# Transposes moved from TensorE to VectorE in a chunk-attention and FFN kernel, with slots of 256 tokens and a new order of the first loads

## The chip, the cores and the metric

The kernel runs on one core of a Trainium2 chip. The metric is the device time of one execution in microseconds (us). A run counts as slow when it took over 1.5 % longer than the fastest of its kernel. Each set of runs was made beside runs of the kernel before on the same chip.

## The reference

Attention is taken within chunks of 64 tokens, for 8 batches, 8 heads, 576 tokens and a head size of 64. The result, as 4608 tokens of 512, goes through a multiplicative FFN.

```python
scores = scale * np.matmul(q_c, k_c.transpose(0, 1, 2, 4, 3))   # 64 x 64 per chunk and head
attn = softmax(scores)
x = matmul(attn, v_c)            # then 4608 x 512
a = x @ w1                       # 512 -> 1024
b = x @ w2
h = a * b @ w3                   # 1024 -> 1024
return h @ w_out                 # 1024 -> 512
```

Both kernels form `w3o = w3 · w_out` once (1024 x 512) and then `(a * b) @ w3o`. They work in bf16, with f32 sums.

## The kernel before

It works in slots of 128 tokens. TensorE turns q, k and x with transposes against an identity, in 64x64 pieces. VectorE copies the turned pieces out of the PSUM tiles that TensorE wrote (`qkT<-pa`, 691 ns each for 128x1024; `xt<-pb`, 424 ns for 128x512).

```python
def do_slot(xu=None, tu=None, su=None, pu=None):        # cut
    if xu is not None:
        ...  tr(xv[half[g], r, n, :], xn[...], ident[half[r], half[r]])   # x: 16 transposes
    if tu is not None:
        ...  tr(tv[half[g], r, s, n, :], qk[...], ident[half[r], half[r]])  # q and k
    if su is not None:
        ...  mm(sv[...], lhsT=qkT[half[r], ci, 1, ...], rhs=qkT[half[r], ci, 0, ...])  # scores
    if pu is not None:
        ...  mm(pb[...], lhsT=e[half[t], ...], rhs=vbuf[...])             # values
    ...
    nc.scalar.activation(e, pa, Exp, scale=scale)
    nc.vector.tensor_copy(qkT_t[tu], tv)
    nc.vector.tensor_copy(xt[...], xv)
    nc.vector.reciprocal(rc, pv[..., D:D + 1]); nc.vector.tensor_mul(xn, pv[..., 0:D], rc)
```

The loads and the front come in this order: w3 and w_out first, with `w3o` formed as they land, and q, k of the first slots between; then w1 and w2; then a and b.

```python
load_w3(0, 1); ...; load_w(wo, ...); load_to(1); ...; load_w3(6, 8)
for w, ap in ((w1, moe_w1), (w2, moe_w2)): ...load_w(...)
load_to(5); load_v(1); load_to(9)
do_w3T(0); do_w3T(1); do_w3o(0); do_slot(tu=0); do_w3o(1); do_slot(tu=1, su=0)   # cut
...
do_w3o(7)
... # then do_a, do_b, do_o with slots placed between
```

The softmax here doesn't subtract the row's maximum and nothing guards it: scores larger than these inputs give would overflow.

## Time and profile before

| | before |
|---|---|
| time, median of 3 (lowest to highest) | 271.62 us (270.75 to 272.07) |
| span of the profiled execution | 270.6 us |
| TensorE, VectorE, ScalarE, GpSimd busy | 90, 45, 34, 35 % |
| first `a` matmul | 43.06 us |

A busy share is an average over the whole span. The row of 40 slices is therefore the first thing to read (slices are counted from 0). The prediction below shows that row, the chain of waits for the first 66 us, and the steady stage. A piece is a start, a length and what filled it; "issue" is time in which TensorE waited for nothing that the profile shows.

```profile
76.56 1.60 issue
...
83.06 1.03 issue
```

### The profile page before, as it was taken

To read this page: it belongs to the slowest core of one execution; us is meant where nothing else is said; L and a number is where in the kernel's file an instruction comes from. 1 tells how busy PE (TensorE), PEld (TensorE's weight loads), DVE (VectorE), ACT (ScalarE), POOL (GpSimd) and SP (SyncE) were. 2 spreads that over 40 slices of the span, in tenths; PEclk is the share of its full clock that TensorE was granted. 3 is DMA by queue.
4 is the path that set the end of the run, shared out by engine and by line. 5 is a ranking of instruction groups with operands and counts; after the bars stand their busy time and mean duration, and the time that the engine had idled before them with its cause. 6 is when DMAs were issued, how large, how long until landed. Compare 5 with 4: busy or idle time off the path is not lost.

```text
span 270.6 us, 8708 instructions
## 1 busy us (share of the span) xinstructions
PE 242.6 (90%) x3896; PEld 127.0 (47%) x3936; DVE 121.4 (45%) x235; ACT 91.2 (34%) x161; POOL 93.9 (35%) x113
## 2 busy tenths in 40 slices
PE   1198599999867999999999999999999999999994
PEld 1135454445655655454444454444444544444441
DVE  1113560364556546775555445555454454332210
ACT  1003125322433343443433344433433343233331
POOL 8484327988857077555422520000000000000000
PEclk9999799999999999999999999999999999999998
DMA  5999999999999999999997991211111111111223
GB/s 87 166 175 169 210 204 158 156 156 202 200 157 142 65 124 155 172 77 151 115 95 84 102 143 45 76 43 41 41 41 41 41 41 70 47 41 39 78 78 118
DMA packets 121620, 29.39 MB, mean 109 GB/s; under 512 B 112880, under 2 KB 115952, under 8 KB 121584
## 3 DMA queue, kind: packets, MB, share of 16 engines
q0 software_dynamic: 116400, 19.41, 94.3%
q1 hardware_dynamic: 5184, 9.44, 9.4%
q8 instruction: 31, 0.51, 0.8%
q14 instruction: 5, 0.04, 0.0%
HBM read 38.80 MB, written 9.44 MB: 178 GB/s over the span
## 4 chain that ended last, share of the span: by engine, by line
PE 78%; DMA 10%; issue 3%; DVE 3%; POOL 2%; ACT 2%; ACTq 0%; POOLq 0%
PE a_ps L59 22%; PE b_ps L59 21%; PE o_ps L59 21%; DMA w_76<-in_moe_w_dram 4%; DMA wo<-in_moe_w_out_dram 4%; PE pa L62 3%; PE pb L62 3%; PE wp L59 3%; DMA out_dram<-o_sb 2%; PE pa L59 2%; PE pb L59 2%; DVE qkT L165 1%; POOL qk L65 1%; DVE xn L175 1%; PE w3tp L62 1%
## 5 line engine op out<-in xcount | busy, mean ns | idle before, releaser
L202 DVE TENSOR_TENSOR ab<-a_sb,b_ps 128x512 bf16<-128x512 f32 (+1 forms) x80 | 50.1, 630 | 57.4 <-PE b_ps L59 52.3
L59 PE MATMUL b_ps<-xt,w_75 128*128 128x512 bf16 (+1 forms) x316 | 74.1, 357 | 0.8 <-ACT o_sb L214 0.3
L59 PE MATMUL a_ps<-xt,w_74 128*128 128x512 bf16 (+1 forms) x294 | 72.3, 357 | 1.6 <-issue 0.5
L59 PE MATMUL o_ps<-w3o,ab 128*128 128x512 bf16 x283 | 66.7, 379 | 0.5 <-issue 0.3
L194 ACT COPY a_sb<-a_ps 128x512 f32<-128x512 f32 (+1 forms) x80 | 43.4, 543 | 49.8 <-PE a_ps L59 47.4
L65 POOL DMA_DIRECT2D qk<-in_q_dram x40 | 34.1, 854 | 46.7 <-PE pa L59 21.9
L59 PEld LDWEIGHTS <-w_75 128*128 128x128 bf16 x320 | 31.1, 98 | 31.4 <-issue 0.8
L214 ACT COPY o_sb<-o_ps 128x512 f32<-128x512 f32 x36 | 21.1, 586 | 66.8 <-PE o_ps L59 62.1
L59 PEld LDWEIGHTS <-ab 128*128 128x128 bf16 x288 | 27.6, 98 | 32.6
L59 PEld LDWEIGHTS <-w_74 128*128 128x128 bf16 x320 | 28.6, 98 | 26.4
L65 POOL DMA_DIRECT2D qk<-in_k_dram x40 | 34.2, 858 | 5.6 <-DMA w_76<-in_moe_w_dram 3.6
L165 DVE COPY qkT<-pa 128x1024 bf16<-128x1024 bf16 x36 | 24.9, 691 | 20.1 <-PE pa L62 13.6
L168 DVE COPY xt<-pb 128x512 bf16<-128x512 bf16 x36 | 15.3, 424 | 40.8 <-PE pb L59 38.1
L160 ACT ACTIVATE e<-pa 128x512 bf16<-128x512 f32 x36 | 21.5, 598 | 28.9 <-PE pa L59 27.1
L175 DVE TENSOR_TENSOR xn<-pb,rc 128x512 bf16<-128x512 f32 x36 | 24.8, 690 | 1.0
L59 PE MATMUL wp<-wo,w3T 128*128 128x512 bf16 x59 | 16.6, 427 | 6.4 <-DMA wo<-in_moe_w_out_dram 5.4
L62 PE MATMUL pa<-ident,qk 64*64 64x64 bf16 x1152 | 16.2, 196 | 1.5 <-issue 1.0
L62 PEld LDWEIGHTS <-qk 64*64 64x64 bf16 x1152 | 12.9, 111 | 6.0 <-issue 5.8
L62 PEld LDWEIGHTS <-xn 64*64 64x64 bf16 x576 | 7.5, 108 | 16.0 <-issue 9.9
L62 PE MATMUL w3tp<-ident,w_76 128*128 128x128 bf16 x64 | 6.4, 265 | 9.5 <-DMA w_76<-in_moe_w_dram 9.5
L233 ACT CAST w3o<-wp 128x512 bf16<-128x512 f32 x8 | 4.7, 586 | 29.9 <-PE wp L59 29.9
L62 PE MATMUL pb<-ident,xn 64*64 64x64 bf16 x576 | 11.6, 199 | 1.9 <-DVE xn L175 1.7
(27 smaller groups left out, 93.6 us busy)
## 6 DMA issues: line engine op xcount, KB each, us to landing
out_dram<-o_sb SPq DMA_DIRECT2D x36, 256.0 KB, 2.9
qk<-in_q_dram POOLq DMA_DIRECT2D x32, 128.0 KB, 6.5
qk<-in_k_dram POOLq DMA_DIRECT2D x32, 128.0 KB, 6.4
vbuf_80<-in_v_dram POOLq DMA_DIRECT2D x6, 288.0 KB, 8.5
vbuf_81<-in_v_dram POOLq DMA_DIRECT2D x6, 288.0 KB, 6.8
vbuf_82<-in_v_dram POOLq DMA_DIRECT2D x4, 288.0 KB, 7.0
w_76<-in_moe_w_dram POOLq DMA_DIRECT2D x4, 256.0 KB, 7.9
wo<-in_moe_w_out_dram POOLq DMA_DIRECT2D x1, 1024.0 KB, 10.6
```

The costliest lines, as they stand in the source:

```text
L59: return inorder(nc.tensor.matmul(*a, **kw))
L62: return inorder(nc.tensor.transpose(*a, **kw))
L65: return inorder(nc.gpsimd.dma_start(dst, src))
L160: nc.scalar.activation(e[:].rearrange("p r m c q -> p r (m c q)"), pa[:, :, 0:HW], Exp, scale=scale, bias=0.0)
L165: nc.vector.tensor_copy(qkT_t[tu][:].rearrange("p r s n t -> p r (s n t)"), tv.rearrange("p r s n t -> p r (s n t)"))
L168: nc.vector.tensor_copy(xt[:, :, xu * UT:(xu + 1) * UT].rearrange("p n (r t) -> p r n t", r=2), xv)
L175: nc.vector.tensor_mul(xn[:], pv[:, :, :, 0:D], rc.to_broadcast([P, 2, NHP, D]))
L194: nc.scalar.copy(a_t[j][:, 0:n], a_ps[:, 0:n])
L202: nc.vector.tensor_mul(ab_t[t][:, j, 0:n], a_t.pop(j)[:, 0:n], b_ps[:, 0:n])
L214: nc.scalar.copy(o_sb[:], o_ps[:])
L233: nc.scalar.copy(w3o[:, ko, :], wp[:])
```

## The change

The intent has three parts. First, TensorE's transposes go away: VectorE turns q, k, x (and w3) by 32x32 blocks in one instruction each, and the index order of the tiles is chosen so that blocks suffice. Second, slots become "pairs" of 256 tokens and every PSUM tile has two banks, in a ring of four. Third, the front is turned round: two pairs of q, k, v come first, then w1 and w2 by quarters, and a and b are formed while w_out and w3 load; later, a and b run two stages behind the values. The diff, cut to its core:

```diff
-    ident = consts.tile([P, P], bf, name="ident")
+    def psum(name):
+        return ps.tile([P, 2, 512], f32, tag="p", name=name)        # bufs=4
...
-                            tr(tv[half[g], r, s, n, :], qk[...], ident[half[r], half[r]])
-            nc.vector.tensor_copy(qkT_t[tu][:]..., tv...)
+        inorder(nc.vector.transpose(
+            qkT_t[p][:, s].rearrange("p e h (y t) -> p h t e y", t=2),
+            qk_t[p][:, s].rearrange("p h (t e y) -> p h t e y", t=2, e=2)))
...
+                for i in range(NB):                                  # scores, 32-row blocks
+                    mm(s_t[p][half[i % 2], i // 2, h * CH:(h + 1) * CH],
+                       lhsT=qkT[blk[i], 1, e, h, :],
+                       rhs=qkT[blk[i], 0, e, h, :], start=(e == 0), stop=(e == 1))
...
-    load_w3(0, 1)
-    load_w(wo, moe_w_out, 0, DM)
-    ...
+    load_to(1)
+    load_w12(0); load_w12(1); load_w12(2)
+    load_to(2)
+    load_w12(3)
+    load_to(4)
+    load_wo()
+    load_w3(0, DF // BL // 2); load_w3(DF // BL // 2, DF // BL)
+    load_to(6)
...
+    T_(0); S_(0); T_(1); P_(0); N_(0); X_(0); S_(1); P_(1); N_(1); X_(1)
+    for j in range(2):
+        do_ab(0, j)(); do_ab(1, j)()
+    do_ab(0, 2)()
+    T_(2); S_(2); do_ab(1, 2)(); P_(2); N_(2); do_ab(0, 3)(); X_(2); do_ab(1, 3)()
+    T_(3); do_ab(2, 0)(); S_(3); ...        # and so on to pair 4
+    for j in range(4):
+        do_ab(4, j)(); do_w3T(j)
+    T_(5); do_w3o(0); do_w3o(1); ...
```

T turns q and k, S is scores and exp, P values, N the division by the sum, X turns x. One `do_ab` is a quarter of a and b of a pair: 16 matmuls of 256 columns, a copy on ScalarE, and the product on VectorE, which the call `()` places.

## The prediction

> **What bounds the kernel now.** I read the page first: the busy shares and the 40 slices (6.77 us each).
>
> ```profile
> span 270.6 us, 8708 instructions
> ...
> PE 242.6 (90%) x3896; PEld 127.0 (47%) x3936; DVE 121.4 (45%) x235; ACT 91.2 (34%) x161; POOL 93.9 (35%) x113
> ...
> PE   1198599999867999999999999999999999999994
> ...
> DMA  5999999999999999999997991211111111111223
> ```
>
> TensorE is the bound from slice 12 on; VectorE and ScalarE have more than half of their time free. The loss is at the front and in slices 10 and 11, where the DMA row stands at 9. So next the chain of waits, in order of time, for the first 66 us:
>
> ```profile
> 3.04 10.65 DMA wo<-in_moe_w_out_dram
> ...
> 18.61 11.30 DMA w_76<-in_moe_w_dram
> ...
> 43.06 4.53 PE a_ps L59 x21
> ```
>
> The first `a` matmul starts at 43.06 us: the kernel first loads w3 (w_76 here) and w_out and forms w3·w_out. Then the steady part, in the timeline of TensorE (start, length, group):
>
> ```profile
> 159.65 1.89 PE L59 MATMUL o_ps<-w3o,ab 128*128 128x512 bf16 x8
> 161.47 0.32 PE L62 MATMUL pb<-ident,xn 64*64 64x64 bf16 x16
> 161.61 0.43 PE L62 MATMUL pa<-ident,qk 64*64 64x64 bf16 x32
> 161.87 0.31 PE L59 MATMUL pa<-qkT 64*64 64x64 bf16 x16
> 161.99 0.32 PE L59 MATMUL pb<-vbuf_82,e 64*64 64x65 bf16 x16
> 162.24 1.04 PE L59 MATMUL a_ps<-xt,w_74 128*128 128x512 bf16 x3
> 163.12 1.03 PE L59 MATMUL b_ps<-xt,w_75 128*128 128x512 bf16 x4
> 163.98 1.03 PE L59 MATMUL a_ps<-xt,w_74 128*128 128x512 bf16 x4
> ```
>
> No gap: from 163.12 to 163.98 four matmuls of 512 columns take 0.86 us, 215.9 ns each. The eight `o` matmuls are issued by 161.38 (159.65 + 8 x 0.2159), the next `a` starts at 162.24: an attention slot of 128 tokens costs TensorE 0.86 us for 80 small matmuls, 48 of them transposes. From start to start these take 8 to 9 ns each ((161.87 - 161.61)/32 = 8.1), in all 0.65 us; the other 0.2 us is at entry (0.09) and exit (0.12). The 256-column form, which becomes the only one for a and b, is in the same view:
>
> ```profile
> 72.14 0.60 PE L59 MATMUL b_ps<-xt,w_75 128*128 128x256 bf16 x4
> ...
> 73.01 0.60 PE L59 MATMUL b_ps<-xt,w_75 128*128 128x256 bf16 x4
> ```
>
> Eight of them in 0.87 us: 109 ns each. Last, the groups, for what VectorE and the DMA queue pay:
>
> ```profile
> L202 DVE TENSOR_TENSOR ab<-a_sb,b_ps 128x512 bf16<-128x512 f32 (+1 forms) x80 | 50.1, 630 | 57.4 <-PE b_ps L59 52.3
> ...
> L65 POOL DMA_DIRECT2D qk<-in_q_dram x40 | 34.1, 854 | 46.7 <-PE pa L59 21.9
> ...
> L165 DVE COPY qkT<-pa 128x1024 bf16<-128x1024 bf16 x36 | 24.9, 691 | 20.1 <-PE pa L62 13.6
> L168 DVE COPY xt<-pb 128x512 bf16<-128x512 bf16 x36 | 15.3, 424 | 40.8 <-PE pb L59 38.1
> ```
>
> [...]
>
> **The change, part by part.**
>
> *TensorE.* Removed: 1152 + 576 transposes of q, k and x and 64 of w3. The matmuls that remain are cut smaller: scores of 256 tokens are 64 matmuls on 32-row blocks (before 32), values 64 on 32-column blocks (before 32). At the old 8.1 ns, 128 of them are 1.04 us; there are three changes of mode (128 to 64x32, to 32x64, to 128) at about 0.1: 0.32. Estimate 1.36 us for 256 tokens, against 2 x 0.86 = 1.72. Over 18 pairs -6.5 us. The w3 transposes: 64 at some 60 ns, -3.8. a and b: before 512 at 215.9 ns and 128 at 109.2 = 124.5; after 1152 at 109.2 = 125.8, +1.3. o (288 x 215.9 = 62.2) and w3·w_out (64 x 215.9 = 13.8) stay. Sum before 124.5 + 62.2 + 13.8 + 3.8 + 36 x 0.86 = 235; after 125.8 + 62.2 + 13.8 + 18 x 1.36 = 226. So the removed transposes alone are worth 9 us.
>
> *VectorE.* Estimates [...]: a q or k transpose (1024 elements) 1.22 us, an x transpose (512) 0.69, a w3 one 1.22. A pair then costs 2 x 1.22 + 2 x (0.20 + 0.69) for reciprocal and scaling + 2 x 0.69 + 4 x 0.69 = 8.4 us; in all 18 x 8.4 + 8 x 1.22 = 161 us, from 121. In the steady stage TensorE needs 1.36 + 64 x 0.1092 + 16 x 0.2159 = 11.8 us, so VectorE at 8.4 lies beside it. I followed one stage through the built order: values and scores, normalising and turning the values, four a,b groups with the next q and k between, then o. With a and b two stages behind, x was turned a stage earlier; o's ScalarE copy (1.02 us, as 512 elements are 586 ns and 256 are 373) ends just inside the 1.36 us of small matmuls before its PSUM slot is wanted. No wait is left, or one of 0.1 us.
>
> *Loads.* A q or k issue is 131 KB and 0.86 us, and from 41 to 62 us POOL issues nearly without a pause while the stretch moves 157 GB/s; the weight stretch (34 to 41 us) moves 203. So I take the small loads to be held by issuing. After, a q or k issue copies 256 tokens in the same 1024 runs, now twice as long: four issues or 3.5 us for a pair of 786 KB, 224 GB/s. Then 203 GB/s holds, 3.9 us for a pair and 1.3 for a weight quarter of 262 KB.
>
> *The front.* The first load lands 3.6 us after its issue at 1.26 (from before). Then, estimated: q0, k0 at 5.0 and 6.3, pair 1 at 11.5, the first quarters of w1 and w2 at 14, the last at 26, pairs 2, 3, 4 at 23, 30, 33, w_out 39, w3 49. VectorE turns q0, k0 until 7.6; scores, exp, values until 10.7; it turns pair 1 until 11.5, scales pair 0 until 13.4 and turns it until 15. So a and b start at about 15 instead of 43 us, and form while w3 loads. But in this front everything alternates on two engines in program order, and TensorE waits for VectorE: for q and k of pair 2, which stand behind a product on VectorE (3.4 us), of pair 3 and for x of pair 2 (2.5), of pair 4 (2), others 0.7: 8.6 us, and the first matmuls run at 427 ns for 512 columns, as w3·w_out does in before from 13.7 to 17: 1.7 more.
>
> *Sum.* Start 15; 20 groups of a,b for pairs 0 to 4 at 1.75 = 35; three pairs' attention 4.1; waits 10.3: 64.5. w3·w_out, pair 5's attention and o(0): 18.6: 83. Stage 6 (scores, a,b, two o) 14.6, stage 7 8.3: 106. Ten stages of 11.8: 224. The last values, a,b and o: 11.2, then a,b 7.0 and two o 6.9: 249. Before, the last matmul group ends at 266.76 and the span at 270.6, a tail of 3.84 that stays: 253. The median of before is 1 us above its page: 254; I take 253, since the waits at the front are rounded up.
>
> **Rivals.** (1) The block transposes run at half the assumed rate, because their rows are strided. Then VectorE needs some 12 us in a stage of 11.8 and becomes the bound, and the front grows by about 6: 266 to 270. [...] (2) Small matmuls on 32-row or 32-column tiles don't overlap as the 64x64 ones do: at 16 ns a pair costs 1 us more, 18 in all: 270. For it: twice as many, each with its own weight load[...]. (3) Loads stay at 157 GB/s: w3 lands at 62 instead of 49 while it is wanted at 58: +4. The w3 and w_out loads go to 32 partitions each, which nothing in the trace tells of. (4) The front overlaps better than I have it and the waits behind VectorE are short: 246.
>
> **Range and chances.** Rival 4 sets the low end, rival 3 with a little of 1 or 2 the high end: 244 to 264. Faster by over 2% means below 266.2; only rival 1 or 2 in full prevents it, about one in ten together. Slower needs both.
>
> **What would show it.** The first a,b group near 15 us; transposes of 1024 elements near 1.22 us and of 512 near 0.69; VectorE busy about 161 us; a stage of 11.8 us late in the run without gaps; 1.36 us between the last o and the first a,b matmul; gaps before the scores of pairs 2, 3, 4 ended by VectorE. A transpose above 1.8 us, or more than 2 us of small matmuls in a stage, makes the prediction wrong, as would a first a,b group after 22 us.

The 1.22 us for turning 1024 elements, and with it the 8.4 us of a pair and the 161 us in all, were an estimate: the trace of before has no such instruction and does not show its rate. The nearest that was measured there is the product of L202 over 128x512, 684 ns with the forms kept apart, against the 0.69 us used for 512 elements.

## The result, and the profile after

The changed kernel took 268.58 us (median of 4 runs, 266.13 to 269.19). The kernel before took 271.41 us in the same rounds (4 runs). The ratio is 0.9867, with a 95 % interval of 0.9817 to 0.9916. Here and below a ratio is taken from the fast runs of the same rounds, so it is not quite the ratio of the medians quoted. By the 2 % bar this counts as the same time. 253 was predicted, with a range of 244 to 264: the prediction was wrong by 15.6 us.

The page of the changed kernel, in the rows that answer to those of before: the busy shares, the slices (of 6.68 us), the instruction queue, and five groups (count, then busy us and mean ns of one).

```profile
span 267.3 us, 8283 instructions
...
PE 234.8 (88%) x3791; PEld 170.2 (64%) x3808; DVE 154.6 (58%) x231; ACT 84.0 (31%) x114; POOL 84.5 (32%) x112
...
PE   0369477974899999999999999999999999999993
...
PEclk9999979997999999999999999999999999999998
DMA  8999999999999979799989791202202020210204
...
q8 instruction: 30, 0.49, 0.8%
...
L188 DVE TENSOR_TENSOR ab<-a_sb,ab_ps 128x512 bf16<-128x512 f32 x72 | 48.4, 673 | 56.4 <-ACT a_sb L187 56.3
...
L129 DVE STREAM_TRANSPOSE qkT<-qk 128x1024 bf16<-128x1024 bf16 x36 | 46.1, 1297 | 3.2 <-DMA qk<-in_q_dram 3.0
...
L170 DVE STREAM_TRANSPOSE xt<-xn 128x512 bf16<-128x512 bf16 x36 | 23.3, 686 | 0.0
...
L58 PE MATMUL pv<-vbuf,e 64*32 64x96 bf16 x1152 | 14.0, 215 | 8.4 <-issue 6.1
```

From slice 11 on TensorE is full, and its busy time fell by 7.8 us. Slices 0 to 10 are mostly thin: TensorE works early now, but with holes. The clock row has two dips, in slices 5 and 9. The last line says that the values waited 6.1 us for "issue", which means for nothing that the profile shows.

The timeline of TensorE shows the front, and a steady stage below it. Columns: start, length, group, and in brackets the idle time before it and what ended that.

```profile
17.12 0.65 PE L58 MATMUL pv<-vbuf,e 64*32 64x96 bf16 x33 [1.27 <-issue]
17.70 11.53 PE L58 MATMUL ab_ps<-xt,w 128*128 128x256 bf16 x80
33.00 0.86 PE L58 MATMUL s_ps<-qkT 32*64 32x64 bf16 x64 [3.77 <-DVE qkT L129]
33.79 3.35 PE L58 MATMUL ab_ps<-xt,w 128*128 128x256 bf16 x16
37.07 0.69 PE L58 MATMUL pv<-vbuf,e 64*32 64x96 bf16 x61
39.27 0.22 PE L58 MATMUL pv<-vbuf,e 64*32 64x96 bf16 x3 [1.51 <-issue]
39.42 3.67 PE L58 MATMUL ab_ps<-xt,w 128*128 128x256 bf16 x32
...
60.04 0.68 PE L58 MATMUL pv<-vbuf,e 64*32 64x96 bf16 x60
64.07 0.27 PE L58 MATMUL pv<-vbuf,e 64*32 64x96 bf16 x4 [3.35 <-issue]
64.27 5.22 PE L58 MATMUL ab_ps<-xt,w 128*128 128x256 bf16 x32
70.35 7.16 PE L58 MATMUL ab_ps<-xt,w 128*128 128x256 bf16 x64 [0.87 <-DVE xt L170]
77.35 2.97 PE L58 MATMUL w_ps<-wo,w3T 128*128 128x512 bf16 x12
...
154.66 0.72 PE L58 MATMUL pv<-vbuf,e 64*32 64x96 bf16 x64
155.32 0.71 PE L58 MATMUL s_ps<-qkT 32*64 32x64 bf16 x64
155.96 7.16 PE L58 MATMUL ab_ps<-xt,w 128*128 128x256 bf16 x64
162.95 3.62 PE L58 MATMUL o_ps<-w3o,ab 128*128 128x512 bf16 x15
166.50 0.72 PE L58 MATMUL pv<-vbuf,e 64*32 64x96 bf16 x64
```

The steady stage is as predicted: 166.50 - 154.66 = 11.84 us (predicted 11.8), 155.96 - 154.66 = 1.30 us for values and scores (predicted 1.36), no gap. The front is not: w3·w_out starts at 77.35 us where 64.5 was worked out, 12.9 us late, and from there to the end nothing is lost. Values stop three times in mid-burst on "issue" (1.27, 1.51 and 3.35 us), behind 31 of 64 matmuls of pair 1, at 61 of 64 of pair 2, at 60 of 64 of pair 4. And 16 a,b matmuls take 3.35 us at 33.79, where 16 take 1.92 in full clock (at 32.43 in the run "warm" below).

What these stops are, the records of the DMA packets tell. The queue q8 that the page calls "instruction" moved 30 packets of 16384 bytes (0.49 MB). The page counts 7599 instructions of TensorE (3791 matmuls and 3808 weight loads), 253 for each packet; 30 times 256 would be 7680. So I took each packet for a block of some 256 of TensorE's instructions. I set the start of each packet against TensorE's records, both from the trace, and counted TensorE's own instructions (a weight load and a matmul are two) up to each stop:

```
kernel   instructions   packet of   TensorE    from packet to
         before stop    16 KB at    goes on    going on
after        446          14.79       17.12       2.33
after        956          36.86       39.27       2.41
after       1722          61.58       64.07       2.49
before      1982          75.71       78.17       2.46
before      2238          81.68       84.09       2.41
```

Each stop ends 2.3 to 2.5 us after such a packet starts. With 66 added (one constant, chosen to fit), the counts are 512, 1022, 1788, 2048 and 2304, within 4 of multiples of 256. Counted by TensorE's records in the trace, semaphore records among them, no constant is needed: the three stops of the changed kernel come behind record 449, 961 and 1729, which are 2 x 256 and 3 x 256 apart. The three stops last 6.1 us together, and 21, 32 and 35 packets of the loads were in flight at the start of the three instruction packets. So theory A was: **TensorE runs out of its instruction block**, because 256 instructions are used up in a burst of attention (128 for the scores, 128 for the values of a pair in 0.65 us each) sooner than the next block comes through the loads. How long a block takes can be read off too. From the moment at which the records pass such a boundary to the start of the next packet it is 2.2 to 4.0 us at the seven boundaries of the first 65 us, with 21 to 36 load packets in flight; some 2.4 us later TensorE could go on.

The half speed is in the granted clock: two stretches of 3.41 us at 0.5, at 33.35 and 64.07, after the idle times of 3.77 and 3.35 us. The idle time in front of a stretch was not always that long: it was 2.77 us in pad128 (stretch at 50.98) and 1.97 in gate5 (at 38.74), two of the runs below.

Rival theories were: **B**, the stops come from something in the values themselves or their buffers, not from where the block ends; **C**, the loss is VectorE's order alone (the wait of 3.77 us at 33.00) and the clock that falls behind it; **D**, the early a and b are not worth anything, and the front loses what it gains however it is fed. The first two were settled; D was not.

### The profile page after: what moved, and what is told of

Read it like the earlier page. It is cut to its first block, busy times and chain, and to the rows that moved or that the text cites. A ratio compares the mean times of both kernels' runs of the same rounds, so it can differ in the third digit from the quotient of the medians.

```text
span 267.3 us, 8283 instructions
## 1 busy us (share of the span) xinstructions
PE 234.8 (88%) x3791; PEld 170.2 (64%) x3808; DVE 154.6 (58%) x231; ACT 84.0 (31%) x114; POOL 84.5 (32%) x112
## 4 chain that ended last, share of the span: by engine, by line
PE 79%; DMA 6%; DVE 5%; POOL 5%; issue 3%; ACT 1%; ACTq 0%; POOLq 0%
PE ab_ps L58 42%; PE o_ps L58 23%; PE w_ps L58 5%; DMA w<-in_moe_w_dram 4%; PE pv L58 4%; PE s_ps L58 4%; DVE qkT L129 3%; DMA qk<-in_q_dram 2%; POOL w L61 2%; POOL qk L61 1%; DVE xt L170 1%; POOL vbuf L61 1%; DVE ab L188 1%; ACT a_sb L187 1%; ACT o_sb L200 0%
## 5 line engine op out<-in xcount | busy, mean ns | idle before, releaser
L58 PE MATMUL ab_ps<-xt,w 128*128 128x256 bf16 x1152 | 135.3, 280 | 2.6 <-DVE xt L170 2.6
L58 PEld LDWEIGHTS <-w 128*128 128x128 bf16 x1152 | 113.8, 100 | 19.9 <-DVE xt L170 3.4
L188 DVE TENSOR_TENSOR ab<-a_sb,ab_ps 128x512 bf16<-128x512 f32 x72 | 48.4, 673 | 56.4 <-ACT a_sb L187 56.3
L187 ACT COPY a_sb<-ab_ps 128x512 f32<-128x512 f32 x72 | 42.1, 585 | 97.7 <-PE ab_ps L58 97.7
L129 DVE STREAM_TRANSPOSE qkT<-qk 128x1024 bf16<-128x1024 bf16 x36 | 46.1, 1297 | 3.2 <-DMA qk<-in_q_dram 3.0
L61 POOL DMA_DIRECT2D vbuf<-in_v_dram x40 | 33.8, 857 | 19.6 <-PE pv L58 14.3
L200 ACT COPY o_sb<-o_ps 128x1024 f32<-128x1024 f32 (+1 forms) x19 | 18.3, 968 | 49.6 <-PE o_ps L58 49.6
L58 PE MATMUL s_ps<-qkT 32*64 32x64 bf16 x1152 | 13.6, 199 | 15.9 <-DVE qkT L129 15.9
L166 DVE TENSOR_TENSOR xn<-pv,rc 128x512 bf16<-128x512 f32 x36 | 24.9, 692 | 1.2
L145 ACT ACTIVATE e<-s_ps 128x1024 bf16<-128x1024 f32 x18 | 18.4, 1024 | 21.0 <-PE s_ps L58 21.0
L58 PEld LDWEIGHTS <-qkT 32*64 32x64 bf16 x1152 | 11.5, 111 | 18.6 <-DVE qkT L129 17.0
L170 DVE STREAM_TRANSPOSE xt<-xn 128x512 bf16<-128x512 bf16 x36 | 23.3, 686 | 0.0
```

The lines of the kernel that those rows point to most:

```text
L58: return inorder(nc.tensor.matmul(*a, **kw))
L61: return inorder(nc.gpsimd.dma_start(dst, src))
L129: inorder(nc.vector.transpose(qkT_t[p][:, s].rearrange("p e h (y t) -> p h t e y", t=2), qk_t[p][:, s].rearrange("p h (t e y) -> p h t e y ...
L145: inorder(nc.scalar.activation(e_t[p][:].rearrange("p u h q -> p u (h q)"), s_t.pop(p)[:], Exp, scale=scale, bias=0.0))
L166: inorder(nc.vector.tensor_mul(xn_t[p, u][:], pv[:, :, :, 0:D], rc.to_broadcast([P, 2, 4, D])))
L170: inorder(nc.vector.transpose(xt[:, :, t0:t0 + UT].rearrange("p o (m y) -> p m o y", y=BL), xn_t.pop((p, u))[:].rearrange("p r (c n) (z o) ...
```

## The experiments

Twelve sets of runs were made, two of them repeats. All gave correct results. w3·w_out start is the first `w_ps` matmul in the profiled run; half-clock stretches are counted in pieces of 3.41 us between 25 and 95 us, behind the cold start (in the changed kernel the first 25 a,b matmuls, from 17.70 to 23.0 us, start 213 ns apart; from 23.2 us on they start 109 apart).

| run | us, median (lowest to highest) | ratio to before [95 %] | w3·w_out at | "issue" in front of s_ps, pv, ab_ps | half-clock stretches |
|---|---|---|---|---|---|
| changed kernel | 268.58 (266.13 to 269.19) | 0.9867 [0.9817, 0.9916] | 77.4 | 6.1 | 2 |
| pad64 | 261.75 (261.24 to 262.02) | 0.9624 [0.9594, 0.9655] | 69.2 | 1.4 | 1 |
| pad128 | 265.05 (263.81 to 266.20) | 0.9733 [0.9682, 0.9783] | 74.5 | 4.2 | 3 |
| pad30 | 262.14 (261.95 to 262.38) | 0.9639 [0.9623, 0.9655] | 70.5 | 1.7 | 1 |
| warm | 260.00 (259.78 to 260.81) | 0.9567 [0.9535, 0.9600] | 68.1 | 1.5 | 0 |
| gate5 | 264.33 (263.17 to 265.69) | 0.9723 [0.9678, 0.9769] | 73.9 | 3.6 | 2 |
| order_a | 264.08 (260.22 to 264.70) | 0.9602 [0.9522, 0.9682] | 72.7 | 8.1 | 3 |
| order_a_pad64 | 255.78 (254.50 to 256.18) | 0.9372 [0.9334, 0.9409] | 63.8 | 1.2 | 1 |
| order_b | 254.98 (254.10 to 256.52) | 0.9353 [0.9300, 0.9405] | 63.8 | 1.8 | 0 |
| order_b again | 254.44 (254.32 to 254.76) | 0.9358 [0.9344, 0.9372] | 62.6 | 1.7 | 0 |
| w3_first | 271.42 (270.56 to 273.04) | 0.9960 [0.9916, 1.0005] | 16.3 | 1.6 | 4 |
| w3_first_b | 260.66 (260.24 to 260.89) | 0.9574 [0.9544, 0.9604] | 16.4 | 0 | 1 |
| w3_first_b again | 262.89 (one run, state unknown) | none | 16.3 | 0.2 | 2 |

(The kernel before took 271.41 us beside the changed kernel, 271.8 beside pad64, pad128, warm and gate5, 271.91 beside pad30 and the repeat of order_b, 272.8 beside the orders and w3_first, 271.87 beside w3_first_b. Two of order_a's four runs were slow, and its last three columns are from a slow one.)

### pad64: every block boundary moved by 64 instructions

Thirty-two tiny matmuls on constants (64 TensorE instructions) stand before everything else, while TensorE would wait for the first q and k anyway. Nothing reads their result.

```diff
+    def pad(n):
+        t = psum("pad")
+        for _ in range(n):
+            mm(t[0:BL, 0, 0:BL], lhsT=vbuf[0][0:BL, 0, 0, D:VW],
+               rhs=vbuf[0][0:BL, 0, 0, D:VW], start=True, stop=True)
+    pad(32)
     load_to(1)
```

> 32 dummy 32x32 matmuls at the very start, before anything is loaded: 64 more TensorE instructions, which shift every later block of 256 instructions by 64. Theory A (the three stops of 1.3, 1.5 and 3.35 us inside the values of pairs 1, 2 and 4 are waits for the next block of 256 TensorE instructions, which comes about 6.3 us after the last block was begun while the loads keep the queues full): the stops leave these three places; with the new phase at most one of about 0.3 us is left at pair 1, so w3*w_out begins near 70 instead of 77.4 us and the time falls by 5 to 8 us, to about 262. Theory B (the stops belong to these instructions: a v load, a PSUM slot or small matmuls as such): the three stops stay where they are and the time stays within 1.5 us of 268.

The time fell to 261.75 us, and w3·w_out starts at 69.2. The waits of TensorE (engine, line and what it waited for; us in total, times, longest) have no values on "issue" any more; what is left stands in front of the last of pair 1's 64 scores. It is 1.2 us, where about 0.3 was expected at pair 1:

```profile
PE s_ps L58 <- DVE qkT L129: 13.5, 5, 6.1
...
PE s_ps L58 <- issue: 1.2, 1, 1.2
```

The kernel does more work and is 7 us faster. The values did not change. Their buffers did, by one place: the dummies take one tile of the ring in PSUM, so every later tile moves on by one. But pad30, pad64 and pad128 all move the ring by this one tile and stop in different places, so with the two runs below B falls. One of the two half-clock stretches went with the long stop at pair 4.

### pad128: the same, twice as far

```diff
+    pad(64)
```

> The same with 64 dummy matmuls, a shift of 128 instructions. Theory A: the stops in the values of pairs 1, 2 and 4 are gone, but new ones stand inside the scores of pair 1 (about 1.6 us) and at the end of the values of pair 3 (about 3 us), where none was; time about 264 to 267. Theory B: stops at pairs 1, 2 and 4 as before, none at the other two places, 268.

It took 265.05 us. The stops came where the boundaries now are:

```profile
PE pv L58 <- issue: 2.8, 1, 2.8
...
PE s_ps L58 <- issue: 1.4, 1, 1.4
```

The stop in the values is now pair 3's, a gap of 2.98 us between weight loads after instruction 1466 (1466 + 66 = 1532), and the other is in the scores of pair 1. The same dummies twice over cost 3.3 us against pad64, and only the place of the boundary differs. Three stretches of half clock (30.50 to 37.33 and 50.98 to 54.40) are part of that.

### gate5: fewer loads in flight when pair 4's block is asked for

The loads of pair 5 and later are held back until pair 4's values are scaled, by one column that VectorE writes into pair 5's tile.

```diff
     load_w3(DF // BL // 2, DF // BL)
-    load_to(6)
 ...
     N_(4)
+    qk_t[5] = io.tile([P, 2, H, 2 * D], bf, tag="qk", bufs=6, name="qk")
+    inorder(nc.vector.memset(qk_t[5][:, :, 0, 0:1], 0.0))
+    load_to(6)
```

> The loads of pair 5 and later are held back until pair 4's values have been scaled, by a VectorE write of one column into pair 5's buffer, so that no load is in flight around 57 to 61 us. Theory A with its second half (the block comes late because the loads fill the same queues): the block wanted in pair 4's values is fetched about 1.5 us after the last one was begun instead of 3.9, as late in the run, where no load is in flight; the stop of 3.35 us shrinks below 1.5 us or goes, with it the half-clock window after it; w3*w_out begins 3 to 5 us earlier; the time is about 264, unless pair 5's loads then come late for the w3*w_out stage (they need 4 us and are wanted 15 us later). If blocks always come that slowly after a burst: the stop stays at 3.3 us and the time at 268.

264.33 us. The blocks in question started at 59.68 and 63.20 with no load packet in flight, and pair 4's stop shrank from 3.35 to 0.36 us, with the same instructions at the same boundaries:

```profile
62.17 0.22 PE L58 MATMUL pv<-vbuf,e 64*32 64x96 bf16 x4 [0.36 <-issue]
```

The sum over the whole run, as us in total, times and longest:

```profile
PE pv L58 <- issue: 3.6, 3, 2.0
```

What is left beside it is pair 1's (1.3) and pair 2's (2.0, before 1.5). From passing the boundary to the packet's start it was 0.94 and 1.03 us at these two blocks, and 2.5 to 4.0 at the five before them in the same run, with 18 to 38 load packets in flight. So both halves of theory A hold in the one case tried: TensorE stopped where the boundary was, and the block's packet started later, by 1.5 to 3 us, when loads were in flight.

### warm: TensorE kept busy while it waits for VectorE

Fifteen 512-column matmuls on data that are there fill the 3.77 us wait in front of pair 2's scores.

```diff
     do_ab(0, 2)()
+    warm(15)        # 15 x mm(t[:, 0, :], lhsT=w1[:, 0, 0:P], rhs=xt[:, 0:2, 0:PT])
     T_(2)
```

> 15 dummy matmuls of 512 columns in the gap of 3.8 us before the scores of pair 2, nothing waits for them. If the slow a,b group after the gap (3.29 us instead of 1.77) is the granted clock falling to half after TensorE stood idle, that group takes 1.8 us, the half-clock window at 33.35 us is gone from the trace, and w3*w_out begins 1.5 us earlier; the time falls by about 1.5 us to 267 (the shift of 30 instructions may move a stop of theory A by some tenths). If the group is slow for its operands (xt just turned, weights just landed), it stays at 3.3 us and the time stays.

It took 260.00 us, a gain of over 8 us where 1.5 was expected. The half-clock stretch is gone: the first a,b group behind pair 2's scores takes 1.92 us instead of 3.35.

```profile
27.84 3.40 PE L58 MATMUL warm<-xt,w 128*128 128x512 bf16 x15
31.80 0.71 PE L58 MATMUL s_ps<-qkT 32*64 32x64 bf16 x64 [0.55 <-DVE qkT L129]
32.43 1.92 PE L58 MATMUL ab_ps<-xt,w 128*128 128x256 bf16 x16
34.28 0.72 PE L58 MATMUL pv<-vbuf,e 64*32 64x96 bf16 x64
```

But the stop in pair 2's values is gone as well, and pair 4's is 0.23. The fifteen dummies are 30 instructions: they moved the boundaries, and the block's packet started at 30.47 instead of 36.86. The experiment mixed two causes; alone it tells nothing about the clock's worth.

### pad30: the same 30 instructions, without the warm-up

```diff
+    pad(15)
     load_to(1)
```

> 15 dummy 32x32 matmuls (30 TensorE instructions) before everything else, so that every later block boundary comes 30 instructions earlier, as behind the warm-up of the run before, but with no long matmuls in the gap before the scores of pair 2. It tells the two effects of the warm-up run apart. Theory A (instruction blocks): the block that ran out in the values of pair 2 is now asked for before the wait for VectorE at about 30.5 us, so that stop (1.5 us) and the one of pair 4 (3.35 us, and the half-clock stretch after it, 1.65 us) go or shrink below 0.5, while the half-clock stretch at 33 to 37 us stays: about 261.5 us, w3 times w_out at 70 to 71. Then the clock was worth about 1.5 us in the warm-up run (260.0). Rival (the clock was the cause of the whole gain there): this run stays at 267 to 269 us.

262.14 us, with w3·w_out at 70.5 and a half-clock stretch at 32.50, as expected under A. The waits keep pair 1's stop and 0.3 of pair 4's:

```profile
PE pv L58 <- issue: 1.7, 2, 1.4
```

So 30 instructions' shift gives some 6.4 us of the warm run's gain (268.58 - 262.14), and the clock about 2.1 (262.14 - 260.00; on two chips, where the runs of the kernel before differ by 0.1). In the profiled runs 0.8 us of this is the cold start (the first five a,b groups take 11.09 us in pad30, 10.30 in warm), which the warm-up cannot have changed. C as the whole cause falls; the clock is a part of it.

### order_a and order_a_pad64: VectorE's order, and the boundary again

The calls of the front are put in another order, found with a small model of the queues that knew nothing of instruction blocks: q and k of pairs 2, 3 and 4 are turned before the products that kept them waiting. The same instructions, no dummies; order_a_pad64 adds `pad(32)`.

```diff
-    do_ab(0, 2)()
-    T_(2)
+    m[0, 1] = do_ab(0, 1)
+    do_T(2, 1)
+    m[1, 1] = do_ab(1, 1)
+    m.pop((0, 1))()
+    m[0, 2] = do_ab(0, 2)
+    do_T(2, 0)
+    m.pop((0, 2))()
     ... # and so on to pair 4, products placed apart from their matmuls
```

> The instructions of the front unchanged in number and loads, but reordered: the turning of q and k of pairs 2, 3 and 4 and of x of pairs 2 and 3 stands ahead of products on VectorE that are not yet wanted. If TensorE's waits behind VectorE's program order (3.8, 0.9, 1.0, 0.9, 1.0, 0.9 us before scores and a,b of pairs 2 to 4) were the prediction's full account of the front, these 8.5 us go, with the half-clock window after the first: w3*w_out near 67 us, time near 258. With theory A on top (blocks of 256 TensorE instructions about 6.3 us apart while loads run), a denser front runs into the next block sooner: the stops grow from 6.1 to about 8.5 us, w3*w_out begins near 73 us, and the time is only 263 to 265.

> The same order behind 32 dummy matmuls that shift the blocks by 64 instructions. Theory A: the phase leaves about 3 us of stops instead of 8.5; w3*w_out begins near 64 us, where the prediction had it (64.5), and the time is 255 to 258, about 5 us under the run with the dummies alone (261.75). If the order is worth nothing beside the blocks: 261 to 262.

order_a took 264.08 us, and its spread is wide: two runs (264.70 both) count as slow, being over 1.5 % above its fastest, and the profiled one is one of them, so its profile is read only for where TensorE stops. By the ratio of the fast runs (0.9602) it took some 262 us, a little less than the 263 to 265 expected. VectorE's waits shrank as meant (10.8 us from 15.9), but the stops grew to 8.1:

```profile
PE s_ps L58 <- DVE qkT L129: 10.8, 3, 8.4
PE pv L58 <- issue: 8.1, 3, 3.4
```

With 64 instructions in front the very same order took 255.78, all four runs fast. By the ratios of fast runs (0.9602, from two runs, and 0.9372) the shift is worth 2.3 % of the kernel before, some 6 us. A better order for VectorE made the bursts come closer together and so ran into the boundaries harder.

### order_b: an order that avoids both, and its repeat

An order chosen with the boundaries in mind, without dummies: by my count of instructions the boundaries behind pair 1 fall into a,b groups (32 instructions in 1.77 us) and not into values (128 in 0.65 us).

```diff
-    X_(1)
-    for j in range(2):
-        do_ab(0, j)()
-        do_ab(1, j)()
-    do_ab(0, 2)()
-    T_(2)
+    do_X(1, 0)
+    m[0, 0] = do_ab(0, 0)
+    do_X(1, 1)
+    m[1, 1] = do_ab(1, 1)
+    m.pop((0, 0))(); m.pop((1, 1))()
+    do_T(2, 0)
+    m[0, 2] = do_ab(0, 2)
+    m[1, 2] = do_ab(1, 2)
+    do_T(2, 1)
     S_(2)
     ...
```

> No dummies: another order of the same front, chosen with the block phase in mind, so that bursts of small matmuls stand apart (a,b groups of other pairs between them). Theory A: stops about 3 us, w3*w_out near 65 us, time 255 to 259. If stops belong to bursts whatever their phase, it is no better than the first reordering: 263 to 265.

254.98 us, ratio 0.9353: it beats both kernels, and is the best version. Its slices (6.34 us each) and clock show a front without the dip in clock:

```profile
span 253.7 us, 8301 instructions
...
PE   0359779999999999999999999999999999999992
...
PEclk9999999999999999999999999999999999999998
```

It was sent once more with the runs of pad30. That run was to be a padded form; the unpadded file went in under the padded label, and the first half sentence of what is on record for it is a slip. It is a repeat and nothing else:

> Mistaken entry guard: this text is replaced below; order b again, unchanged, to be compared on the same chip with its padded form: 254 to 257 us.

254.44 us on another chip; 0.9358 against 0.9353. How order_b does with shifted boundaries is therefore not known.

### w3_first: the third part of the change undone, badly

w3 and w_out are loaded first again and multiplied before a and b; the rest of the change stays.

```diff
-    load_to(1)
-    load_w12(0)
-    ...
-    load_wo()
     load_w3(0, DF // BL // 2)
+    load_wo()
+    load_to(0)
     load_w3(DF // BL // 2, DF // BL)
+    load_to(1)
+    for i in range(4):
+        load_w12(i)
     load_to(6)
+    for j in range(4): do_w3T(j)
+    do_w3o(0); do_w3o(1)
     T_(0); S_(0)
     ...
```

> The third part of the change undone: w3 and w_out are loaded first and w3*w_out is formed before a and b, as before the change, with everything else kept (turning on VectorE, 256 tokens, 2-bank ring, a,b two stages behind values). Estimate from the measured load rate: w3 and w_out fill the first 20 us, the first a,b group starts near 31 us, the stages are dense from about 46 us, each with 11.8 us for 416 TensorE instructions, so that blocks are never short. If the front's loss comes from a,b and attention of five pairs running at once on short blocks while everything loads: 246 to 252. If the early a,b are worth what the change meant them to be, this loses against the change's kernel: 268 or more.

271.42 us: the expectation was missed by 19 us. The chain of waits tells why:

```profile
38.89 0.73 PE pv L58 x64
39.62 13.96 PE ab_ps L58 x112
54.82 2.47 DVE qkT L129 x2
57.34 0.71 PE s_ps L58 x64
58.04 3.56 PE o_ps L58 x16
63.81 1.21 DVE xt L170 x2
65.02 2.35 DVE qkT L129 x2
```

My order turned q and k of pair 2 only behind seven of the eight products of pairs 0 and 1, and then let TensorE wait through whole chains on VectorE for two more stages. It tested my order as much as the third part, so it counts for neither theory.

### w3_first_b: the third part undone, without those waits

The same loads in the main, q and k of the next pair turned ahead, and steady stages from pair 3 on.

```diff
     for j in range(4, 8): do_w3T(j)
     T_(1); do_w3o(2); S_(1)
+    T_(2)
     do_w3o(3); P_(1); N_(1); X_(1)
     do_ab(0, 0)(); do_ab(0, 1)()
     S_(2)
     do_ab(0, 2)()
+    do_T(3, 0)
     do_ab(0, 3)()
+    do_T(3, 1)
     ... # from pair 3 on: P(s-1), S(s), N, X, four a,b of pair s-2 with T(s+1) between, o
```

> The third part of the change undone once more (w3 and w_out loaded and multiplied first, a and b only when w1 and w2 have come behind them), now without the serial waits on VectorE that spoiled the first try: q and k of the next pair are turned before they are wanted, and the stages from pair 3 on are the steady ones of the changed kernel. From the first try: w3 times w_out can start at 16.3 us and takes 15; a and b should start at 37 to 39 us; behind that 126 us of a and b, 62 of o, 16 pairs at 1.3 and a tail of 3.8 remain: 250 to 252 us with no gap, 253 to 257 with one or two stops of 1.5 to 3 us at instruction blocks. Theory A (the early a and b of the changed kernel bring nothing that its front doesn't lose again): this kernel is at least 10 us faster than the changed one (268.6) and level with its best order (254.4 to 255.0). Rival (a and b early is what the change lives from, and the first try showed its true worth): 266 us or more.

260.66 us, above the expected 250 to 257: a and b start at 41.57 and not at 37 to 39. Two waits behind VectorE are again in part of my ordering, 3.96 us for the second half of w3, which VectorE turns only after it has scaled and turned pair 0, and 2.00 us before the scores of pair 3:

```profile
30.98 0.60 PE L58 MATMUL w_ps<-wo,w3T 128*128 128x512 bf16 x1 [3.96 <-DVE w3T L208]
...
41.57 3.67 PE L58 MATMUL ab_ps<-xt,w 128*128 128x256 bf16 x32
...
52.12 0.71 PE L58 MATMUL s_ps<-qkT 32*64 32x64 bf16 x64 [2.00 <-DVE qkT L129]
```

It was sent once more for one look, again under a label that says padded though the file is the same (the text on record says so):

> The kernel of the run before it, unchanged, as one look only: the same 250 to 257 us, and the same places of the stops at instruction blocks (if it has any), since the blocks are counted from the start of the program and nothing in it moved. A stop at another place, or of another length by over 1 us, would speak against theory A.

262.89 us in its one run (of unknown state). No stop on "issue" was longer than 0.3 us in either execution, so nothing here spoke against theory A; most of the 2 us more is the clock. Both executions idle 2.0 us at about 50; in one the a,b groups behind it run at full clock, in the other a stretch of 3.41 us at half clock begins at 52.35. The chain of the first, then of the repeat:

```profile
52.83 7.09 PE ab_ps L58 x64
```

```profile
53.55 8.18 PE ab_ps L58 x64
```

So whether an idle time of 2.0 us costs the clock differs from run to run of one kernel. And the main reading: with the first two parts of the change alone, 260.66 against 271.87, 11 us faster. The third part as written turns that into 268.58, 8 us worse; order_b, which has it too, took 254.4 to 255.0, 6 us better. These 6 us don't show what early a and b are worth, for w3_first_b still has the two waits. By the landing records w3's second half was there at 26.25 and k of pair 3 at 50.06. Turned at once, two tiles of w3 would have been ready at some 28.7 and that k at 51.3, so 2.3 and 0.8 us of the waits are order and the rest is loads. The half clock behind the first wait (14 matmuls in 4.50 us, 15 of the same group in 3.40) may have cost 1.3 us more. So some 3 to 4.4 of the 6 us are my order, by this estimate, and D stays open: neither theory's number was met (at most 258.6, or 266 or more), and no run sets a good order with w3 first against a good order with a and b first.

## Why the prediction was wrong

**Right: TensorE's sum and the steady stage.** The stage measured 11.84 us against 11.8, values and scores 1.30 against 1.36. From start to start the 64 a,b matmuls of a stage take 162.95 - 155.96 = 6.99 us, the 109.2 ns each that were used; the chain of waits gives a group of 64 as 7.09 us, 110.8 ns each. From the start of w3·w_out to the end the sum of the prediction holds: 253 - 64.5 = 188.5, measured 267.3 - 77.35 = 190.0.

**Right: VectorE.** Turning 1024 elements took 1.22 to 1.30 us (1297 ns in the mean of q and k, 1.218 in the median of w3) against 1.22, 512 elements 0.686 against 0.69, and VectorE was busy 154.6 us against 161. Rivals 1 and 2 of the prediction (half-rate transposes, 16 ns for small matmuls) are refuted by the same lines.

**Right in size: the waits behind VectorE.** "TensorE waits for VectorE ... 8.6 us": the timeline and chain have 3.8, 0.9, 1.0, 0.9, 1.0 and 0.9, in all 8.5. The parts agree too: 3.8 us for pair 2 (listed 3.4), 1.9 for pair 3's scores and x of pair 2 (2.5), 1.9 for x of pair 3 and pair 4's scores (2), 0.9 for x of pair 4 (0.7).

**Wrong, but without cost: the loads.** By the landing records they came later than estimated: the last quarter of w2 at 29.8 us (26), pairs 3 and 4 at 34.5 and 39.1 (30, 33), w_out at 44.2 (39), w3 at 55.5 (49). VectorE turned w3 from 73.5 on, so TensorE did not wait for it: rival 3 of the prediction came true by about half, and cost nothing.

**Wrong: the step "Start 15; ... waits 10.3: 64.5".** The front took 12.9 us more than this; the rest of the 15.6 us is 1.5 us behind the front and 1.3 by which the median lies above the profiled span (the 253 was a span). The terms, as measured:

- The list of waits had no term for TensorE's own instructions. The stops in the values of pairs 2 and 4 are 1.51 + 3.35 = 4.9 us on the path (pair 1's 1.27 is in the next point). pad64, pad128 and pad30, with 64, 128 and 30 instructions in front, show that they follow the boundary of 256 instructions; in gate5, with no load in flight there, the longest of them was 0.36 us.
- The first a,b group was put at 15 us and came at 17.70: 2.7 us, of which 1.27 is the stop in pair 1's values. The rest stems from pair 1: its k landed at 11.76 and was turned until 13.1, while the prediction has the pair land at 11.5 and turned until 11.5, which leaves no time for turning k. The first quarters of w1 and w2 were late as well (14.8 and 17.1 by the landing records, against 14), but the a,b group follows pair 1's values without a gap, so it did not wait for them.
- Half rate was given 1.7 us, for one cold start. The first five groups took 11.5 us against 5 x 1.75 = 8.75, so the cold start alone cost 2.7; in the chain of waits the groups behind the scores of pair 2 and behind the values of pair 4 took 3.29 and 3.42 us against 16 x 110.8 ns = 1.77, which is 1.5 and 1.65 more. Together 5.9, or 4.2 more than predicted. The second stretch I take for a result of the 3.35 us stop: in pad64, without that stop, it was gone too. The cold start differs between runs with the same five groups: 11.5 us here, 10.0 in order_a's profile.

That is 4.9 + 2.7 + 4.2 = 11.8 of 12.9 us. Of the other 1.1, 0.4 is 20 groups at 1.77 instead of 1.75 and 0.5 the attention of three pairs (4.6 us in the chain, against 4.1); the rest is not assigned. The step that failed is thus the list of waits: it had no place for TensorE's instructions. These stops are 6.1 us with pair 1's and 7.8 with the half clock that the longest one brings.

**The failed step can be checked by taking it away.** pad64 moves the boundaries and keeps the order and the loads: w3·w_out starts 8.2 us earlier (69.2; 0.9 of this is a shorter cold start), and the kernel takes 6.8 us less. order_b keeps the predicted work and loads, brings the "issue" to 1.8 us and the half clock behind pair 2 to nothing: w3·w_out starts at 63.8 (predicted 64.5) and the kernel takes 254.98 (predicted 253). But it also shortens the waits of the scores behind VectorE (11.7 us from 15.9 in the listing of waits), and the waits for x that the list counted at 2.6 us are gone. The prediction counted these waits as there to stay, so order_b's near agreement with 64.5 and 253 is in part luck: fewer waits than predicted make up for a later start and for the stops that remain.

**What could have been seen.** The chain of before had the two "issue" pieces shown above; the page gives all of the chain's "issue" as 3 %. I took them for rest. They are at instructions 1982 and 2238, the same kind of stop (they end 2.46 and 2.41 us after a packet starts), in slices 11 and 12 of the row. The prediction named slices 10 and 11 and set them beside a DMA row at 9; but that row stands at 9 from slice 1 to slice 20 and singles nothing out. Why the change loses more by these stops is argued, not tested. Its bursts are no longer than before (80 small matmuls in a slot, now 64 or 128 together). But they stand in a front where a and b now run beside the loads and every stop is on the path. And a block of a,b instructions lasts half as long: 128 matmuls at 109.2 ns are 14.0 us, at 215.9 ns they were 27.6 (an estimate).

## What to carry to other kernels

Count TensorE's instructions, not only its time: here, where small matmuls used up 256 instructions in 1.3 us and a 16 KB block came 4.6 to 6.4 us after a boundary was passed (2.2 to 4.0 to the packet's start, some 2.4 more until TensorE could go on) with 21 to 36 load packets in flight, TensorE stopped with nothing to wait for. A piece called "issue" in the middle of a burst, with a multiple of 256 instructions between one such stop and the next (512 and 768 records in the changed kernel, 256 instructions in the one before), was the sign; the test was to put some dummy instructions in front and see whether the stop moves. And before reading a gain from any experiment that adds instructions, check that it didn't just move such a boundary, as the warm-up run did here (30 instructions alone gave some 6.4 us of it).
